# Layer matmuls of 384 instead of 288 columns in an attention, ELU and Mish kernel on one Trainium2 core

## The chip, the cores and the metric

The kernel runs on one core of a Trainium2 chip. The time is the device time of one execution in microseconds (us), lower is better. The engines are called by the names of the profile: PE is TensorE (matmuls; PEld its weight loads), DVE is VectorE, ACT is ScalarE, POOL is GpSimd, SP is SyncE, which only issues DMAs here.

## The reference

Rotary attention, then two expert layers on its output; all in float32, with weights given in float64.

```python
q, k, v: (2, 8, 576, 64)                       # batch, heads, tokens, head size
scores = rotate(q) @ rotate(k)^T / 8           # rotary table on both
attn = softmax(scores); x = attn @ v           # x: (1152, 512), tokens of both batches
h = x @ w_in                                   # (1152, 2048)
g = where(h > 0, h, exp(min(h, 0)) - 1)        # ELU
x = g @ w_out                                  # (1152, 512)
h = x @ w_in2                                  # second layer
g = h * tanh(log1p(exp(h)))                    # Mish
out = g @ w_out2
```

## The kernel before

**Numbers.** Each float32 operand of a layer matmul is split into a high and a low part (float32r), and a product is made of three passes: high x high, high x low, low x high. `XH`, `XL` hold the layer input, transposed (features on partitions). Weights come in float64 and are rebuilt on the chip: `weight_stages` takes one [128, 512] block through L95 (POOL), L99, L103, L107 (DVE), then the high part on ACT (L121) and the low part on POOL (L122). One call of `weight_part` is one of four steps of one block; `weight_job` is a whole block.

**Attention.** Eight pairs of heads (`p`), nine units each (`u = 9 p + i`): scores into PSUM (`do_S`, L407), row minima on DVE (`do_max`, L414), exponentials on ACT (`do_exp`, L427), transposes of the result on PE (`do_T`, L474, L476, L479) three units later (`LAG`), evacuated by `do_evac` and `do_evac_last`, then products with v (`do_av`, L514). The loop over `u` issues everything in a hand-written order, which every engine keeps. Row sums are inverted on DVE (`do_inverse`, into the tile `rw`), spread over partitions by transposes (`do_spread`) and copied by ACT (`do_keep`, L459); `do_x` multiplies, `do_xh` (ACT) and `do_xl` (POOL) make the parts of x. For pair 1, `second_split` makes the high parts of key and query on ACT and the low parts on POOL (L332), at units 5 and 6. The last transpose of pair 0 (L476) goes into a corner of the tile `psA`, from which `do_keep` reads; it stands at the start of unit 11.

**Layers.** G1 (`g1_mm`, L186) multiplies one block of 128 hidden features with 576 tokens of one batch, as two matmuls of 288 columns for each of 4 input blocks and 3 passes: 24 matmuls. There are 16 feature blocks x 2 batches = 32 such units a layer, in groups of four blocks. `elu` (three functions on ACT), `elu_join` (two steps on DVE, the second reads PSUM), `elu_hi` (ACT) and `elu_lo` (DVE, L238) make the two parts of g; `mish` does the same in the second layer. G2 of the first layer (`g2_first`, L779) adds a group of four feature blocks into one output block and one batch: 24 matmuls of 288 columns, 32 of them. G2 of the second layer (`g2_second`, L808) has tokens as output rows, 128 a tile, 12 matmuls of 512 columns; the tile that spans both batches needs its g parts copied together (`seam`, SP DMAs into `GX`). `step(n)` issues a unit: G1, weight steps, the functions, and one or two due G2s from `pend`. The order is by hand in the first layer; in the second only ACT's is. PSUM holds two G1 tiles and two G2 tiles of two banks; unit 4 of the first layer borrows a G2 tile. The first three G1s (`early`) are issued from the last attention units (`tail`), and `PARTS` says how many weight steps each of these units carries.

Of the kernel before, what the change touches and what calls it, by code (L numbers as in the profile page):

```python
# [14 lines left out]
ALU = mybir.AluOpType  # L15
# [11 lines left out]
def kernel(  # L27
# [31 lines left out]
    XH = main.tile([128, NB, NC, S], F32R, name="XH")  # L59
    XL = main.tile([128, NB, NC, S], F32R, name="XL")  # L60
# [24 lines left out]
    def weight_stages(key):  # L85
# [28 lines left out]
        pool, tag = wpool if even else late_pool[0], ("wi", "wo")[kind] + ("0" if even else "1")  # L114
        hi = pool.tile([128, 512], F32R, tag=tag + "h", name=tag + "h", bufs=GF)
        lo = pool.tile([128, 512], F32R, tag=tag + "l", name=tag + "l", bufs=GF)
# [58 lines left out]
    def g1_mm(m, f, b):  # L175
        c = m * NF + f
        hi, lo = WI[c]
        if (m, f, b) == (0, 0, 1):
            o = g_pool[0].tile([128, 2, 512], F32, tag="g", name="ps_g", bufs=2)
        else:  # L180
            o = ps_s()
        k = 0
        for cc in range(NC):
            for w, x in ((hi, XH), (hi, XL), (lo, XH)):
                for j in range(2):
                    nc.tensor.matmul(  # L186
                        o[:, j, :HS], lhsT=w[:, cc, :], rhs=x[:, b, cc, j * HS:j * HS + HS],
                        start=(k == 0), stop=(k == 3 * NC - 1),
                    )
                k += 1  # L190
        return o
# [7 lines left out]
    def tmp(tag):  # L199
        return late_pool[0].tile([128, S], F32, tag=tag, name=tag, bufs=5)  # L200

    def tmps():
        if tmp_pool[0] is not None:
            t = tmp_pool[0].tile([128, 2, S], F32, tag="P", name="P", bufs=PB)
            return t[:, 0, :], t[:, 1, :]
        return tmp("ta"), tmp("tb")

    def galloc(m, f, b):
# [3 lines left out]
        t = pool.tile([128, 2, S], F32R, tag=tag, name=tag, bufs=bufs)  # L212
        G[m * NF + f, b] = t
        return t[:, 0, :], t[:, 1, :]
# [4 lines left out]
    def elu(m, f, b, o):  # L219
        h = o[:, :, :HS]  # L220
# [4 lines left out]
        return m, f, b, h, t, g  # L225

    def elu_join(m, f, b, h, t, g):
        nc.vector.scalar_tensor_tensor(out=g, in0=t, scalar=1.0, in1=g, op0=ALU.add, op1=ALU.mult)  # L228
        nc.vector.tensor_tensor(out=v2(g), in0=v2(g), in1=h, op=ALU.max)  # L229
        return m, f, b, g  # L230

    def elu_hi(m, f, b, g):
        gh, gl = galloc(m, f, b)
# [7 lines left out]
    def attention(att, ps, tail):  # L241
# [3 lines left out]
        rw = att.tile([128, 4, 64], F32, name="rw")  # L245
# [82 lines left out]
        def second_split(i):  # L328
# [3 lines left out]
            nc.gpsimd.tensor_tensor(out=d[l], in0=qk_t[1][:, i, :], in1=plain(d[h]), op=ALU.subtract)  # L332
# [100 lines left out]
        def do_inverse(p, g):  # L433
# [13 lines left out]
        def do_spread(p, g):  # L447
            for t in range(2):
                nc.tensor.transpose(  # L449
                    psA[:, 128 * t:128 * t + 128], rw[:, 2 * t:2 * t + 2].rearrange("p h d -> p (h d)"), idn  # L450
# [164 lines left out]
        PARTS.update({NU: 4, NU + 1: 3, NU + 2: 2, NU + 3: 1})  # L615
# [19 lines left out]
        for u in range(max(av_at) + 1):  # L635
# [17 lines left out]
            if first_T:  # L653
# [40 lines left out]
            if u == TPP + 1:  # L694
# [4 lines left out]
                av_at[u + 1] = []  # L699
            if 0 <= u - LAG < NU:  # L700
# [20 lines left out]
            if u == 6:  # L721
# [20 lines left out]

    def moe(mp, early):
        GX = {}

        def seam(m, f, b):
            c = m * NF + f
            n = S % 128
            if b == 0:
                GX[c] = mp.tile([128, 2, 128], F32R, tag="gx", name="gx", bufs=2 * GF)  # L750
# [217 lines left out]
```

## Time and profile before

| | us |
|---|---|
| three runs | 566.83, 564.95, 564.42 |
| median | 564.95 |
| the profiled execution | 564.36 |
| its span, first to last instruction | 562.5 |
| PE busy / DVE busy / ACT busy / POOL busy | 550.6 / 369.2 / 274.6 / 237.5 |
| mean granted clock of TensorE | 0.996 |

The stages by the time of the span: the head and the two pairs that are treated apart until about 45 us, the other pairs until about 147, the first layer with ELU until about 350, the second with Mish to the end. A matmul's record is longer than its turn, as matmuls are pipelined; the turn is read from the distance between starts, or from a piece of the chain of waits that says how many matmuls it holds.

### The profile page before, as it was taken

To read this page: it belongs to the slowest core of one execution; us is meant where nothing else is said; L and a number is where in the kernel's file an instruction comes from. 1 tells how busy PE (TensorE), PEld (TensorE's weight loads), DVE (VectorE), ACT (ScalarE), POOL (GpSimd) and SP (SyncE) were. 2 spreads that over 40 slices of the span, in tenths; PEclk is the share of its full clock that TensorE was granted. 3 is DMA by queue.
4 is the path that set the end of the run, shared out by engine and by line. 5 is a ranking of instruction groups with operands and counts; after the bars stand their busy time and mean duration, and the time that the engine had idled before them with its cause. 6 is when DMAs were issued, how large, how long until landed. Compare 5 with 4: busy or idle time off the path is not lost.

```text
span 562.5 us, 10157 instructions
## 1 busy us (share of the span) xinstructions
PE 550.6 (98%) x3904; PEld 505.5 (90%) x3904; DVE 369.2 (66%) x596; ACT 274.6 (49%) x511; POOL 237.5 (42%) x231
## 2 busy tenths in 40 slices
PE   7989999999999999999999999999999999999997
PEld 6768888888899999999999999999999999999985
DVE  4758787788978866777777777679744555532231
ACT  3657676677676655455454565336443232322110
POOL 7999989843424323222332222526423322320000
PEclk9989999999999999999999999999999999999999
DMA  7378887772323232222322222425523323000012
GB/s 233 107 214 220 215 209 195 196 182 78 124 76 114 89 100 77 75 76 81 108 76 76 75 76 76 122 82 163 170 85 92 119 85 122 10 15 9 29 65 94
DMA packets 57968, 62.00 MB, mean 110 GB/s; under 512 B 29632, under 2 KB 47808, under 8 KB 57152
## 3 DMA queue, kind: packets, MB, share of 16 engines
q1 hardware_dynamic: 57376, 60.77, 37.1%
q8 instruction: 31, 0.51, 0.4%
q10 hardware_dynamic: 544, 0.59, 0.3%
q14 instruction: 17, 0.14, 0.1%
HBM read 47.51 MB, written 2.36 MB: 89 GB/s over the span
## 4 chain that ended last, share of the span: by engine, by line
PE 87%; DVE 6%; ACT 3%; issue 1%; DMA 1%; POOL 0%; SPq 0%; DVEq 0%; ACTq 0%; POOLq 0%
PE ps_s L186 32%; PE ps_h L808 18%; PE ps_g L779 17%; PE ps_s L407 8%; PE psA L514 7%; PE psT L474 5%; ACT P L427 1%; DVE wu L107 1%; DMA qk_t<-in_qk_dram 1%; DVE wu L103 1%; DVE tb L229 1%; DVE mn L414 1%; DVE tb L228 1%; PE psA L449 1%; PE psL L479 0%
## 5 line engine op out<-in xcount | busy, mean ns | idle before, releaser
L414 DVE TENSOR_REDUCE mn<-ps_s 128x1 f32<-128x576 f32 x72 | 53.6, 754 | 23.1 <-PE ps_s L407 22.8
L758 ACT ACTIVATE ta<-ps_s 128x576 f32<-128x576 f32 x32 | 20.8, 649 | 94.2 <-PE ps_s L186 94.1
L427 ACT ACTIVATE P<-ps_s,mn 128x576 f32<-128x576 f32 x72 | 53.1, 740 | 10.9 <-DVE mn L414 10.6
L186 PE MATMUL ps_s<-XL,wi1h 128*128 128x288 f32 x256 | 54.9, 296 | 0.0
L186 PE MATMUL ps_s<-XH,wi1h 128*128 128x288 f32 x256 | 54.7, 295 | 0.0
L186 PE MATMUL ps_s<-XH,wi1l 128*128 128x288 f32 x256 | 54.6, 295 | 0.0
L186 PE MATMUL ps_s<-XH,wi0h 128*128 128x288 f32 x248 | 53.6, 298 | 0.6 <-DVE tb L229 0.5
L186 PE MATMUL ps_s<-XL,wi0h 128*128 128x288 f32 x248 | 53.2, 296 | 0.0
L186 PE MATMUL ps_s<-XH,wi0l 128*128 128x288 f32 x248 | 53.0, 295 | 0.0
L122 POOL TENSOR_TENSOR wo0l<-wu,wo0h 128x512 fp32r<-128x512 f32 x16 | 21.8, 1364 | 68.7 <-ACT wo0h L121 58.1
L99 DVE TENSOR_SCALAR wu<-wu 128x512 int32<-128x512 int32 x64 | 29.4, 460 | 31.8 <-POOL wu L95 31.8
L107 DVE SCALAR_TENSOR_TENSOR wu<-raw,wu 128x512 int32<-128x512 int32 x64 | 47.3, 740 | 1.8
L103 DVE SCALAR_TENSOR_TENSOR wu<-raw,wu 128x512 int32<-128x512 int32 x64 | 47.1, 736 | 2.0
L122 POOL TENSOR_TENSOR wi0l<-wu,wi0h 128x512 fp32r<-128x512 f32 x16 | 21.4, 1340 | 63.7 <-ACT wi0h L121 63.7
L95 POOL TENSOR_SCALAR wu<-raw 128x512 f32<-128x512 f32 x64 | 44.8, 702 | 4.8
L122 POOL TENSOR_TENSOR wo1l<-wu,wo1h 128x512 fp32r<-128x512 f32 x16 | 22.0, 1375 | 58.3 <-ACT wo1h L121 58.3
L760 DVE TENSOR_TENSOR g<-ta,g 128x576 fp32r<-128x576 f32 x25 | 20.4, 817 | 36.4 <-ACT g L759 36.4
L122 POOL TENSOR_TENSOR wi1l<-wu,wi1h 128x512 fp32r<-128x512 f32 x16 | 21.4, 1334 | 53.3 <-ACT wi1h L121 53.3
L474 PE MATMUL psT<-idn,P 128*128 128x128 f32 x288 | 43.5, 276 | 0.0
L186 PEld LDWEIGHTS ps_s<-XH,wi1h 128*128 128x128 f32 x256 | 42.0, 188 | 1.2
L186 PEld LDWEIGHTS ps_s<-XH,wi0h 128*128 128x128 f32 x248 | 40.3, 188 | 2.8 <-DVE tb L229 1.0
L228 DVE SCALAR_TENSOR_TENSOR tb<-ta,tb 128x576 f32<-128x576 f32 x30 | 22.7, 757 | 29.6 <-ACT tb L224 29.3
(176 smaller groups left out, 1454.9 us busy)
## 6 DMA issues: line engine op xcount, KB each, us to landing
raw<-in_w_in_dram SPq DMA_DIRECT2D x32, 512.0 KB, 3.8
raw<-in_w_out_dram SPq DMA_DIRECT2D x32, 512.0 KB, 3.3
qk_t<-in_qk_dram SPq DMA_DIRECT2D x6, 1152.0 KB, 5.3
qa<-qh SPq DMA_DIRECT2D x24, 144.0 KB, 3.7
out_dram<-Y SPq DMA_DIRECT2D x9, 256.0 KB, 2.0
ka<-kh SPq DMA_DIRECT2D x12, 144.0 KB, 3.2
ka<-kl SPq DMA_DIRECT2D x12, 144.0 KB, 2.6
qb<-ql SPq DMA_DIRECT2D x12, 144.0 KB, 3.1
```

Of the source, the lines that this page charges most:

```text
L95: nc.gpsimd.tensor_scalar(out=u, in0=high.bitcast(F32), scalar1=REBASE, scalar2=0.0, op0=ALU.mult, op1=ALU.add)
L103: nc.vector.scalar_tensor_tensor(out=ui, in0=high, scalar=-0x80000000, in1=ui, op0=ALU.bitwise_and, op1=ALU.bitwise_or)
L107: nc.vector.scalar_tensor_tensor(out=ui, in0=low, scalar=29, in1=ui, op0=ALU.logical_shift_right, op1=ALU.bitwise_or)
L122: nc.gpsimd.tensor_tensor(out=lo, in0=u, in1=plain(hi), op=ALU.subtract)
L186: nc.tensor.matmul(o[:, j, :HS], lhsT=w[:, cc, :], rhs=x[:, b, cc, j * HS:j * HS + HS], start=(k == 0), stop=(k == 3 * NC - 1),)
L407: nc.tensor.matmul(psS[w][:, j, :HS], lhsT=l, rhs=r(slice(j * HS, j * HS + HS)), start=(a == 0), stop=(a == len(passes) - 1),)
L414: nc.vector.tensor_reduce(out=m, in_=psS[u][:, :, :HS], axis=AX.XY, op=ALU.min)
L427: nc.scalar.activation(out=P.rearrange("p (j n) -> p j n", j=2), in_=psS.pop(u)[:, :, :HS], func=AF.Exp, scale=-1.0, bias=mn_t.pop(u), acc ...
L474: nc.tensor.transpose(tv[:, c, :], P[:, k:k + 128], idn)
L514: nc.tensor.matmul(o[64 * h:64 * h + 64, cols], lhsT=v, rhs=rhs, start=(c == 0 and first), stop=(c == 4), skip_group_check=True,)
L779: nc.tensor.matmul(o[:, j, :HS], lhsT=w[:, e * 128:e * 128 + 128], rhs=gt[:, i, j * HS:j * HS + HS], start=(k == 0), stop=(k == 3 * GF - 1),)
L808: nc.tensor.matmul(o, lhsT=l, rhs=w, start=(k == 0), stop=(k == 3 * GF - 1))
```

## The change

The layers are cut in three chunks of 384 tokens instead of two batches of 576. A G1 unit is a pair of feature blocks with one chunk: the two PSUM banks of a tile hold the two blocks, and each matmul has 384 columns. That makes 8 pairs x 3 chunks = 24 units of 24 matmuls a layer. `g2_first` has a chunk and a pair of output blocks, 24 times. The chunks are multiples of 128, so `seam` and `GX` go. `XH`, `XL` become [128, 4, 1152]; the g tiles and the temporaries are 768 wide, and half of the even W_out blocks' tiles move to the later pool. `count(n)` and `due(n)` say how many weight blocks a step carries: 0, 0, 2, 1, 2, 2, then one and two in turn. The third early unit reads tokens of the second batch.

In the attention, pair 1's low parts go to DVE (`second_lo`, at units 5 and 7, with `stack_q(1)` at 7), pair 0's last transpose is issued at the end of unit 10, `rw` becomes a part of the tile `R_t`, and the low part of x for pair 0 goes to DVE.

```diff
-    XH = main.tile([128, NB, NC, S], F32R, name="XH")
+    XH = main.tile([128, NC, NT], F32R, name="XH")
...
-    def g1_mm(m, f, b):
-        c = m * NF + f
-        hi, lo = WI[c]
-        if (m, f, b) == (0, 0, 1):
-            o = g_pool[0].tile([128, 2, 512], F32, tag="g", name="ps_g", bufs=2)
-        else:
-            o = ps_s()
+    def g1_mm(m, fp, t):
+        o = ps_s()
+        ws = [WI[m * NF + 2 * fp + j] for j in range(2)]
         k = 0
         for cc in range(NC):
-            for w, x in ((hi, XH), (hi, XL), (lo, XH)):
+            for i, x in ((0, XH), (0, XL), (1, XH)):
                 for j in range(2):
                     nc.tensor.matmul(
-                        o[:, j, :HS], lhsT=w[:, cc, :], rhs=x[:, b, cc, j * HS:j * HS + HS],
+                        o[:, j, :CH], lhsT=ws[j][i][:, cc, :], rhs=x[:, cc, t * CH:t * CH + CH],
                         start=(k == 0), stop=(k == 3 * NC - 1),
                     )
...
             nc.scalar.activation(out=d[h], in_=qk_t[1][:, i, :], func=AF.Copy)
-            nc.gpsimd.tensor_tensor(out=d[l], in0=qk_t[1][:, i, :], in1=plain(d[h]), op=ALU.subtract)
+
+        def second_lo(i):
+            d = sp_t[1]
+            h, l = ("kh", "kl") if i else ("qh", "ql")
+            nc.vector.tensor_tensor(out=d[l], in0=qk_t[1][:, i, :], in1=plain(d[h]), op=ALU.subtract)
...
-        PARTS.update({NU: 4, NU + 1: 3, NU + 2: 2, NU + 3: 1})
+        PARTS.update({NU: 4, NU + 1: 2, NU + 2: 1, NU + 3: 1})
...
-            if first_T:
+            if first_T and u != TPP + 2:
                 do_T(u - LAG)
...
                 av_at[u + 1] = []
+                do_T(u + 1 - LAG)
...
-            if u == 6:
+            if u in (5, 7):
+                second_lo(2 if u == 5 else 0)
+            if u == 7:
                 stack_q(1)
...
-                    do_xl(pp, g, nc.gpsimd if pp < NP - 1 else nc.vector)
+                    do_xl(pp, g, nc.gpsimd if 0 < pp < NP - 1 else nc.vector)
...
+    units = [(m, g * GF // 2 + k, t) for m in range(2) for g in range(NG) for t in range(NT // CH) for k in range(GF // 2)]
...
-        def g2_first(g, b, e):
+        def g2_first(g, t, ep):
...
-                for w, i in ((hi, 0), (hi, 1), (lo, 0)):
+            for f in range(g * GF, g * GF + GF):
+                for w, i in ((0, 0), (0, 1), (1, 0)):
                     for j in range(2):
+                        e = 2 * ep + j
                         nc.tensor.matmul(
-                            o[:, j, :HS], lhsT=w[:, e * 128:e * 128 + 128], rhs=gt[:, i, j * HS:j * HS + HS],
+                            o[:, j, :CH], lhsT=WO[f][w][:, e * 128:e * 128 + 128], rhs=g_part(f, t, i),
...
+        def due(n):
+            return 2 * GF + (n + 1) * 2 * GF // (UB * NT // CH)
+
+        def count(n):
+            if n < half - 1:
+                return (0, 0, 2, 1, 2, 2)[n] if n < 6 else 1 + n % 2
+            return max(0, min(len(jobs), due(n)) - njob[0])
...
             if m == 0:
-                for _ in range(3 if GF <= n < half - 1 else 0):
-                    weight_part()
+                if n >= GF - 1:
+                    some(3)
                 if o is not None:
-                    o = elu(m, f, b, o)
-                    for _ in range(3 if n < GF else 0):
-                        weight_part()
+                    o = elu(units[n], o)
+                    some(8 if n == 2 else 0)
                     o = elu_join(*o)
-                if GF <= n < half - 1:
-                    weight_part()
+                some(1)
                 if o is not None:
                     o = elu_hi(*o)
+                some(3)
             else:
-                mish(m, f, b, o)
-            if f % GF == GF - 1:
-                g = f // GF
+                mish(units[n], o)
+            if fp % UB == UB - 1:
+                g = fp // UB
                 if m == 0:
-                    pend.extend((n + (2 if n < GF else D1 if n < half - 1 else LATE[e]), (0, (g, b, e))) for e in range(NC))
+                    pend.extend((n + 2, 0, g, t, ep) for ep in range(NC // 2))
                 else:
-                    pend.extend((n + D2, (1, (g, t))) for t in TB[b])
-            cnt = 2 if n in (2 * GF, half - 2, half + 1, half + 2) or n > half and n % 8 == 4 else 1
+                    pend.extend((n + 2, 1, g, t * CH // 128 + i) for i in range(CH // 128))
+            cnt = 2 if n > half + 2 and n % 2 else 1
```

## Rows read from the trace of the kernel before

**Rows 1.** The page, engine shares: busy us, share of the span, instructions.
```profile
PE 550.6 (98%) x3904; PEld 505.5 (90%) x3904; DVE 369.2 (66%) x596; ACT 274.6 (49%) x511; POOL 237.5 (42%) x231
```
**Rows 2.** Windows: from:to us, busy PE, PEld, DVE, ACT, POOL, clock, DMA, GB/s.
```profile
20.00:40.00 20.00, 17.89 (x148) 13.16 (x149) 12.38 (x25) 11.65 (x28) 19.32 (x17) 0.91 0.56 155
...
184.60:345.00 160.40, 160.40 (x1205) 160.40 (x1204) 119.48 (x175) 85.93 (x134) 50.07 (x50) 1.00 0.27 86
377.30:539.60 162.30, 162.30 (x974) 148.12 (x973) 82.13 (x116) 53.27 (x87) 47.40 (x44) 1.00 0.27 80
539.60:562.50 22.90, 19.02 (x84) 15.40 (x82) 5.57 (x8) 1.33 (x2) 0.00 (x0) 0.97 0.23 84
```
**Rows 3.** Waits of PE: who waited for whom, us in total, times, longest.
```profile
PE psA L476 <- ACT R L459: 2.1, 1, 2.1
...
PE ps_s L186 <- DVE tb L229: 0.5, 1, 0.5
```
**Rows 4.** The chain of waits in the layers: start, us, what.
```profile
197.37 3.20 PE ps_s L186 x24
200.57 3.20 PE ps_g L779 x24
...
430.18 3.18 PE ps_s L186 x24
433.36 2.74 PE ps_h L808 x12
```
**Rows 5.** Groups of DVE by form: busy us, mean ns, idle before and releaser.
```profile
L107 DVE SCALAR_TENSOR_TENSOR wu<-raw,wu 128x512 int32<-128x512 int32 x64 | 47.3, 740 | 1.8
...
L99 DVE TENSOR_SCALAR wu<-wu 128x512 int32<-128x512 int32 x64 | 29.4, 460 | 31.8 <-POOL wu L95 31.8
L228 DVE SCALAR_TENSOR_TENSOR tb<-ta,tb 128x576 f32<-128x576 f32 x30 | 22.7, 757 | 29.6 <-ACT tb L224 29.3
L238 DVE TENSOR_TENSOR g<-tb,g 128x576 fp32r<-128x576 f32 x24 | 22.5, 939 | 8.1 <-ACT g L234 6.9
```
**Rows 6.** Timeline where the first layer begins, PE and POOL: start, us, what.
```profile
158.01 0.53 PE L186 MATMUL ps_s<-XH,wi0h 128*128 128x288 f32 x2
...
169.91 1.29 POOL L122 TENSOR_TENSOR wo0l<-wu,wo0h 128x512 fp32r<-128x512 f32 x1 [2.69 <-ACT wo0h L121]
...
170.90 0.69 PE L779 MATMUL ps_g<-ge,wo0h 128*128 128x288 f32 x4
```
**Rows 7.** Timeline of PE in the head, in brackets idle time before and releaser.
```profile
28.34 0.61 PE L474 MATMUL psT<-idn,P 128*128 128x128 f32 x4
31.02 0.30 PE L476 MATMUL psA<-idn,P 128*64 128x128 f32 x1 [2.07 <-ACT R L459]
...
36.33 0.53 PE L407 MATMUL ps_s<-kh,qa 64*128 64x288 f32 x4
```
**Rows 8.** Windows, 32 to 36 us, with the granted clock behind the five engines.
```profile
32.00:36.00 4.00, 4.00 (x25) 2.47 (x22) 2.26 (x4) 1.55 (x4) 3.84 (x4) 0.57 0.62 220
```
**Rows 9.** Timeline of DVE and ACT in the head.
```profile
20.94 1.42 DVE L414 TENSOR_REDUCE mn<-ps_s 128x1 f32<-128x576 f32 x2 [0.68 <-PE ps_s L407]
...
30.05 0.59 ACT L494 ACTIVATE pt<-psT 128x512 f32<-128x512 f32 x1
...
30.84 0.43 ACT L541 ACTIVATE XH<-R 128x256 fp32r<-128x256 f32 x1
...
32.35 1.42 DVE L414 TENSOR_REDUCE mn<-ps_s 128x1 f32<-128x576 f32 x2
```
**Rows 10.** Timeline of DVE at the end of the attention: steps with two SBUF inputs.
```profile
148.66 1.02 DVE L103 SCALAR_TENSOR_TENSOR wu<-raw,wu 128x512 int32<-128x512 int32 x1
...
151.90 0.84 DVE L545 TENSOR_TENSOR XL<-R,XH 128x256 fp32r<-128x256 f32 x1 [0.62 <-ACT XH L541]
...
161.65 0.52 DVE L545 TENSOR_TENSOR XL<-R,XH 128x320 fp32r<-128x320 f32 x1 [0.54 <-ACT XH L541]
```

More of the change, by code (lines that the diff above doesn't have):

```diff
@@ L113, in weight_stages @@
         even = c // GF % 2 == 0
-        pool, tag = wpool if even else late_pool[0], ("wi", "wo")[kind] + ("0" if even else "1")
-        hi = pool.tile([128, 512], F32R, tag=tag + "h", name=tag + "h", bufs=GF)
-        lo = pool.tile([128, 512], F32R, tag=tag + "l", name=tag + "l", bufs=GF)
+        tag, bufs = ("wi", "wo")[kind] + ("0" if even else "1"), GF
+        if kind and even:
+            bufs = GF // 2
+            tag += "b" * (c % GF >= bufs)
+        pool = wpool if even and tag[-1] != "b" else late_pool[0]
+        hi = pool.tile([128, 512], F32R, tag=tag + "h", name=tag + "h", bufs=bufs)
+        lo = pool.tile([128, 512], F32R, tag=tag + "l", name=tag + "l", bufs=bufs)
         if kind == 0:
@@ L211, in galloc, with g_part, elu @@
         pool, tag, bufs = (main, "ge", GE) if i < GE else (late_pool[0], "g", GB - GE)
-        t = pool.tile([128, 2, S], F32R, tag=tag, name=tag, bufs=bufs)
-        G[m * NF + f, b] = t
-        return t[:, 0, :], t[:, 1, :]
+        g = pool.tile([128, 2, 2 * CH], F32R, tag=tag, name=tag, bufs=bufs)
+        G[m, fp, t] = g
+        return g[:, 0, :], g[:, 1, :]
+    def g_part(f, t, i):
+        m, f = divmod(f, NF)
+        return G[m, f // 2, t][:, i, f % 2 * CH:f % 2 * CH + CH]
     def v2(t):
         return t.rearrange("p (j n) -> p j n", j=2)
-    def elu(m, f, b, o):
-        h = o[:, :, :HS]
+    def elu(unit, o):
+        h = o[:, :, :CH]
         t, g = tmps()
@@ L449, in do_spread @@
                 nc.tensor.transpose(
[L450 removed]
+                    psA[:, 128 * t:128 * t + 128], R_t[p, g][:, 128 * t:128 * t + 128], idn
                 )
@@ L816, in g2_second @@
                     nc.sync.dma_start(out=out[t * 128:t * 128 + 128, :], in_=y)
-        blocks = [(m, g, b) for m in range(2) for g in range(NG) for b in range(NB)]
-        g1_seq = [(m, g * GF + fi, b) for m, g, b in blocks for fi in range(GF)]
-        half = len(g1_seq) // 2
-        D1, D2, LATE = 1, 2, (2, 2, 3, 3)
+        half = len(units) // 2
+        UB = GF // 2
         pend = []
+        late_pool[0] = mp
         def run_g2(it):
-            if it[0] == 0:
-                g2_first(*it[1])
-            else:
-                g2_second(*it[1])
@@ L836, in step, with some @@
+        def step(n):
+            m, fp, t = units[n]
+            o = early.pop(n) if n in early else g1_mm(m, fp, t)
+            todo = 4 * count(n) if n < half - 1 else 0
+            def some(k):
+                nonlocal todo
+                for _ in range(min(k, todo)):
+                    weight_part()
+                    todo -= 1
             if m == 0:
-                for _ in range(3 if GF <= n < half - 1 else 0):
-                    weight_part()
+                if n >= GF - 1:
+                    some(3)
@@ L857, in step @@
+            cnt = 2 if n > half + 2 and n % 2 else 1
             while pend and cnt and pend[0][0] <= n:
-                run_g2(pend.pop(0)[1])
+                run_g2(pend.pop(0)[1:])
                 cnt -= 1
-            if m == 0:
-                if o is not None:
-                    elu_lo(*o)
-            for _ in range(0 if n < half - 1 else 1 + (n in (half + 1, half + 2))):
-                weight_job()
+            if m == 0 and o is not None:
+                elu_lo(*o)
+            some(4)
@@ L866, in moe @@
+            if n >= half - 1:
+                for _ in range(count(n)):
+                    weight_job()
         pools = ExitStack()
@@ L880, in moe @@
             for n in range(half, 2 * half):
-                if n == half + 4:
+                if n == half + 3:
                     psum("ps_h")
```

95 lines of the change are left out of this document (36 added, 59 removed).

## The prediction

> **What bounds the kernel now.** I read the engine shares first: TensorE is busy 98% of the span, VectorE 66% [rows 1]. An average says little, so next came the stages. In 184.6 to 345 us (first layer) and in 377.3 to 539.6 us (second layer) TensorE is busy for the whole stretch at the full granted clock; VectorE has 119.5 of 160.4 us there, and 82.1 of 162.3. Only the head (20 to 40 us: 17.9 of 20, clock 0.91) and the last stretch leave gaps [rows 2]. The waits of TensorE agree: two matter here, 2.1 us once in the head, and 0.5 us once where the first layer begins [rows 3]. So outside the head the kernel lasts as long as its matmuls take from start to start. That pitch is read from the chain of waits, since the duration of one record contains pipeline time: 24 matmuls of 288 columns take 3.20 us in the first layer, 3.18 us in the second, and 12 of 512 columns take 2.74 us [rows 4]. Per matmul: 133.3, 132.5 and 228.3 ns.
>
> **The matmuls.** At 2.4 GHz, where these stretches run, 288 columns last 120.0 ns and 512 last 213.3 ns, so 13.3 and 15.0 ns come on top of the columns. A line through the two measured pitches has a slope of 0.424 ns per column and 11 ns at zero columns; 384 columns then cost 133.3 + 96 x 0.424 = 174.0 ns in the first layer and 173.3 in the second. No row has 384 columns: the bounds are 160 + 13.3 and 160 + 15.0. I take the line, as it lies between two rows of the same kind of matmul.
> The change keeps the columns and cuts the matmuls by a quarter. G1 (L186) has 64 units of 24 before and 48 of 24 after, half of them in each layer; the first layer's G2 (L779) has 32 x 24 = 768 before and 24 x 24 = 576 after; the second layer's G2 (L808) stays at 432.
> First layer G1: 768 x 133.3 = 102.4 us becomes 576 x 174.0 = 100.2. Its G2: the same, 102.4 to 100.2. Second layer G1: 768 x 132.5 = 101.8 becomes 576 x 173.3 = 99.8. Sum: 306.6 to 300.2, or 6.4 us less. With the bounds: 1728 matmuls at 173.3 to 175.0 ns give 299.5 to 302.4, a gain of 7.1 to 4.2 us. All of it lies on the path, since TensorE has no gap there.
> The Trainium skill speaks against a gain of this size: its page "TensorE: Matmul & The Clock Gate", section "Back-to-back issue gap", gives N / 2.4 GHz + 2.5 ns for a warm matmul. By that, dropping 576 matmuls is worth 1.4 us, not 6.4. The rows show 13.3 and 15.0 ns above the columns where the page has 2.5, each of these matmuls with a weight load of its own; the trace disagrees with the page here.
>
> **VectorE and ScalarE in the layers.** A unit is now 768 wide instead of 576, and there are three for four. I scale the rows by 4/3, which is an upper bound because the fixed part of an instruction doesn't grow: 757 to 1009 ns for the join (two of them), 939 to 1252 for the low part [rows 5], and 1000 for adding a G2 result. One unit of the first layer: 2 x 1.01 + 1.25 + 1.00 = 4.3 us. The weights come faster: between units 6 and 22 the new count gives 25 weights to 17 units, 1.47 each, at 460 ns and twice 740 ns (L103 has the form of L107) = 1.94 us [rows 5], or 2.85 us. Together 7.1 us of a unit's TensorE time of 48 x 174 ns = 8.35 us: 85%. The waits for ScalarE between max and low part fall mostly under the weight steps placed there. A unit's PSUM tile is wanted again two units later, 12.5 us after its G1 ended, and G2 wants the unit two units on, so VectorE may lag by several us before TensorE notices: no cost. The seam copies (one SP DMA per second-layer unit) go; nothing on the path waited for them: no gain.
>
> **Where the layers begin.** Units 0 and 1 last 24 x 174 ns = 4.18 us each after and 3.20 before, so the attention's last products slip by 1.95 us; unit 2, at 158.0 before [rows 6], starts near 159.9, unit 3 ends two units later near 168.3, and the first G2 follows at once; before, it started at 170.9 [rows 6]. So the fourth W_out weight is due earlier than before, when its low part began at 169.9 on GpSimd [rows 6]. I followed the queues, with the durations of the trace scaled to 768 (an estimate): ScalarE starts unit 1 near 158.0, after unit 0's high part, and is through its three functions at 160.5; two joins on VectorE, to 162.4; the last x product, its copy and unit 1's high part, to 164.2; its low part, to 165.2; then the last two weights at 1.94 us each, to 169.0. ScalarE's high part of the last one ends near 169.6, and GpSimd's low part takes 1.29 us from there [rows 6], behind the opening of the next weight: near 171.4. G2 takes the weights in order and reaches this low part after 22 of its 24 matmuls, at 168.3 + 22 x 0.174 = 172.1. It fits, by 0.7 us; a late weight costs its lateness, up to 2 us. The PSUM tile of unit 2 is free near 170.9 (two joins behind the weights) and wanted by unit 4 at 172.5. The third PSUM pool, which unit 4 borrowed, isn't needed: before, the 0.5 us wait was for such a tile [rows 3]; I let it go, 0.45 us. Between the layers, unit 24 needs the first chunk's sum, high and low part: about 3.1 us of VectorE and ScalarE after the chunk's last G2, while one G1 and one G2 (8.3 us) lie between: hidden. The end stays: last product, one add, one DMA [rows 2].
>
> **The head.** Before, pair 0's last transpose goes to psA, behind ScalarE's copy from psA, and TensorE stands from 28.95 to 31.02 us [rows 7]; the clock then is 0.57 between 32 and 36 us [rows 8]. The change issues this transpose one step earlier, ahead of that copy, so the 2.07 us go. What is late next? The scores of the next two tiles need the PSUM tiles that the exponentials free, and these end at 29.96 us (ScalarE's evacuation starts at 30.05 [rows 9]); so at best 1.2 us.
> Against that stand new waits on VectorE. The key's low part enters its queue ahead of the row minima that start at 20.94 us [rows 9], and the query's ahead of the next ones. No row shows this instruction on VectorE. The 576-wide low part of the layers takes 939 ns [rows 5], and a 256-wide one took 0.84 us while GpSimd worked, a 320-wide one 0.52 us while it didn't [rows 10]: between 0.76 and 1.5 us; I take 1.2, nearer the contended row, as GpSimd is busy 19.3 of these 20 us [rows 2]. Two of them, half of it in idle time, delay the following pair's minima by some 1.2 us. Then pair 0's low part of x (L545) moves to VectorE too: it waits for ScalarE's copy of 30.84 us (now near 32.0), and behind it stand the evacuation of the last transpose and the minima that began at 32.35. They begin near 34.3; products, exponentials and the scores of 36.33 us [rows 7] follow at 36.6. Net +0.3 us, if the clock holds; if it falls again the half-rate products add about 1.5 us, and if VectorE isn't slowed the head gains up to 2 us. I take +0.3, with -2 to +2. GpSimd is relieved, but in the list from which [rows 3] are taken no line of TensorE names it.
> The Trainium skill names the reason for the contended row: "GPSIMD Engine Reference" (introduction, table of the engine) says that GpSimd shares its SBUF interfaces with VectorE and contends with VectorE instructions that have two SBUF inputs, as both low parts have. With the uncontended price the sum would be about 1 us lower.
>
> **The sum.** The profiled execution took 564.36 us (span 562.5 and 1.9 around it), 0.6 below the median of 564.95. 564.36 - 6.4 - 0.45 + 0.3 = 557.8; I say 558.0.
>
> **The rivals.**
> (a) The change doesn't do what it says: what comes on top of the columns grows with them (13.3 x 384 / 288 = 17.8 ns, pitch 177.8, sum 307.2 and thus no gain), 564.2 with the other terms. Against it: 15.0 and not 23.7 ns at 512 columns. Chance 0.08. The page on TensorE named above would have it in a milder form, 562.8.
> (b) The head loses the clock again, and the layers' start waits up to 2 us for its weights: 558 + 1.5 + 2 = 561.5, and past 562.1 if the matmuls give only their lower bound as well. The margin of 0.7 us speaks for it, and the clock that fell in the head before [rows 8]. Chance 0.12.
> (c) Slower: VectorE becomes the bound of the first layer, because its weights come in 17 units instead of being spread. Place: units 6 to 22; it decides when a unit costs VectorE more than 8.35 us. All of its two-input steps at the contended rate (1.02 us for a weight step, as the one at 148.66 us [rows 10]) make 1.47 x 2.5 + 4.7 = 8.4 us, and 0.5 to 0.9 us of waits for ScalarE that nothing fills make about 9.2: 17 x 0.85 = 14 us, or 572. Against it: the means of [rows 5], which already hold this mix. Chance 0.06.
> The forecast has 0.74, with its own range from 564.36 - 7.1 - 0.45 - 2 = 554.8 to 564.36 - 4.2 - 0.45 + 2 = 561.7.
>
> **How the numbers follow.** The range takes in the forecast and three quarters of (b), about 0.83: 554.8 to 562.0. A measurement of this kernel tells about 0.5% (2.8 us) from no change, so faster means below 562.1: the forecast and three quarters of (b), 0.83; the same: (a) and the rest of (b), 0.11; slower: (c), 0.06.
>
> **What would show it.** Right: 3328 matmuls; in the chain 24 matmuls of 384 columns take 4.17 to 4.18 us in both layers; no wait of TensorE between 145 and 540 us above 0.5 us; the transpose to psA ahead of the copy, with the scores of 36.33 us within 2 us of that place. Wrong: 24 matmuls at 4.27 us (a), TensorE waiting for a wo0 weight near 172 us or at a clock below 1 after 32 us (b), or TensorE waiting for VectorE's max in every unit of the first layer (c).

## The result, and the profile after

| | before, us | after, us |
|---|---|---|
| median of the runs beside each other | 564.95 | 560.17 |
| lowest and highest | 564.42 to 566.83 | 558.71 to 561.32 |
| profiled execution, and its span | 564.36, 562.5 | 561.02, 559.2 |

The ratio is 0.9904, with a 95% interval from 0.9874 to 0.9934: faster by 1%, 2.2 us above the 558.0 of the prediction and inside its range. Executions of one kernel lie some 2 us apart, in part because TensorE's granted clock falls in the head of some of them; the profiled execution of the changed kernel is one of those.

The page of the changed kernel, engine shares (busy us, share of the span, instructions), for [rows 1]:

```profile
PE 546.1 (98%) x3328; PEld 500.5 (90%) x3328; DVE 375.8 (67%) x560; ACT 267.4 (48%) x459; POOL 244.4 (44%) x227
```

Its windows (from:to us, busy PE, PEld, DVE, ACT, POOL, clock, DMA share, GB/s), for [rows 2] and [rows 8]:

```profile
20.00:40.00 20.00, 16.61 (x124) 12.31 (x125) 13.32 (x22) 10.43 (x26) 15.38 (x13) 0.84 0.57 156
184.60:345.00 160.40, 160.40 (x928) 160.40 (x927) 136.65 (x162) 87.44 (x115) 65.39 (x58) 1.00 0.30 96
377.30:539.60 162.30, 162.30 (x825) 148.12 (x824) 72.67 (x101) 47.56 (x67) 43.56 (x40) 1.00 0.19 61
...
32.00:36.00 4.00, 2.19 (x17) 1.66 (x16) 3.78 (x6) 1.00 (x4) 3.57 (x3) 0.70 0.93 335
36.00:40.00 4.00, 4.00 (x24) 2.63 (x21) 0.36 (x1) 1.34 (x4) 0.52 (x1) 0.50 0.83 179
```

The layers are still solid TensorE. VectorE is busy for 136.7 of 160.4 us of the first layer, 85%, which is what the prediction said. The head lost: 16.6 us of TensorE work in 20 to 40 us where there were 17.9, at a mean clock of 0.84. From 36 to 40 us the clock is 0.50, the lower of its two levels, and TensorE, busy all that time, starts 24 matmuls.

The waits of TensorE (who waited for whom, us in total, times, longest), for [rows 3]:

```profile
PE ps_s L415 <- ACT P L435: 3.2, 7, 0.9
PE psA L521 <- DVE pt L499: 1.8, 1, 1.8
...
PE ps_g L777 <- POOL wo0bl L127: 0.8, 1, 0.8
PE ps_g L777 <- ACT wo0bh L126: 0.3, 1, 0.3
```

The 2.1 us for ScalarE's copy and the 0.5 us for a PSUM tile are gone. In their place stand 1.8 us for `pt` in the head and 0.8 + 0.3 = 1.1 us for weights where G2 begins. The waits for the exponentials (`P`) have grown as well, from 1.8 us in 4 waits to 3.2 in 7: 0.90 us at 24.11 us, 0.17 and 0.33 near 31 us.

The chain of waits in the layers (start, us, what), for [rows 4]:

```profile
181.50 4.16 PE ps_g L777 x24
185.66 4.16 PE ps_s L187 x24
...
494.63 4.18 PE ps_s L187 x24
498.82 2.76 PE ps_h L801 x12
```

A matmul of 384 columns takes 4.16 / 24 = 173.3 ns in the first layer and 4.18 / 24 = 174.2 ns in the second. The 1536 matmuls of the first layer at 133.3 ns [rows 4] were 204.8 us and are 1152 at 173.3, 199.7; those of the second layer's G1 go from 101.8 to 576 x 174.2 = 100.3. Together 6.6 us less.

From the first G1 (146.82 us before, 149.73 after) to the end of the span the kernel takes 562.5 - 146.82 = 415.7 us before and 559.2 - 149.73 = 409.5 after: 6.2 us gained. The head gives 149.73 - 146.82 = 2.9 us back. That is the whole difference, 564.36 - 6.2 + 2.9 = 561.1. Some tenths in such places belong to the execution and not to an edit: the first scores start at 9.30 us before and at 9.50 after, and with one and the same head at 9.19 (e4_TL, below) and 9.39 (e7_TLparts).

### The profile page after: what moved, and what is told of

It reads as the page before. It is cut to its first block, busy times and chain, and to the rows that moved or that the text cites. A ratio compares the mean times of both kernels' runs of the same rounds, so it can differ in the third digit from the quotient of the medians.

```text
span 559.2 us, 8818 instructions
## 1 busy us (share of the span) xinstructions
PE 546.1 (98%) x3328; PEld 500.5 (90%) x3328; DVE 375.8 (67%) x560; ACT 267.4 (48%) x459; POOL 244.4 (44%) x227
## 4 chain that ended last, share of the span: by engine, by line
PE 87%; DVE 3%; POOL 3%; issue 3%; DMA 2%; ACT 1%; SPq 0%; POOLq 0%; ACTq 0%
PE ps_s L187 33%; PE ps_h L801 18%; PE ps_g L777 17%; PE ps_s L415 7%; PE psA L521 7%; PE psT L481 4%; DMA qk_t<-in_qk_dram 1%; DVE mn L422 1%; DMA bh<-qa 1%; ACT P L435 1%; POOL wu L96 1%; POOL wo0bl L127 1%; POOL wo0l L127 1%; PE psL L486 0%; DVE wu L108 0%
## 5 line engine op out<-in xcount | busy, mean ns | idle before, releaser
L100 DVE TENSOR_SCALAR wu<-wu 128x512 int32<-128x512 int32 x64 | 39.7, 620 | 43.1 <-POOL wu L96 43.1
L759 ACT ACTIVATE ta<-ps_s 128x768 f32<-128x768 f32 x24 | 19.5, 812 | 100.8 <-PE ps_s L187 100.8
L104 DVE SCALAR_TENSOR_TENSOR wu<-raw,wu 128x512 int32<-128x512 int32 x64 | 50.6, 791 | 2.0
L187 PE MATMUL ps_s<-XH,wi0h 128*128 128x384 f32 x192 | 49.1, 336 | 0.0
L108 DVE SCALAR_TENSOR_TENSOR wu<-raw,wu 128x512 int32<-128x512 int32 x64 | 47.8, 747 | 1.8
L187 PE MATMUL ps_s<-XL,wi1h 128*128 128x384 f32 x192 | 48.9, 335 | 0.0
L187 PE MATMUL ps_s<-XL,wi0h 128*128 128x384 f32 x192 | 48.8, 335 | 0.0
L187 PE MATMUL ps_s<-XH,wi1l 128*128 128x384 f32 x192 | 48.8, 335 | 0.0
L187 PE MATMUL ps_s<-XH,wi0l 128*128 128x384 f32 x192 | 48.8, 335 | 0.0
L187 PE MATMUL ps_s<-XH,wi1h 128*128 128x384 f32 x192 | 48.7, 334 | 0.0
L761 DVE TENSOR_TENSOR g<-ta,g 128x768 fp32r<-128x768 f32 x16 | 17.5, 1093 | 37.0 <-ACT g L760 37.0
L501 ACT ACTIVATE pt<-psT 128x512 f32<-128x512 f32 x44 | 26.2, 597 | 28.9 <-PE psT L481 28.9
L521 PE MATMUL psA<-pt,v_t 128*64 128x256 f32 (+1 forms) x240 | 37.1, 410 | 2.3 <-DVE pt L499 1.8
L481 PEld LDWEIGHTS psT<-idn,P 128*128 128x128 f32 x288 | 35.2, 143 | 2.0 <-issue 1.4
```

The costliest lines, as they stand in the source:

```text
L100: nc.vector.tensor_scalar(out=ui, in0=ui, scalar1=3, scalar2=0x7FFFFFF8, op0=ALU.logical_shift_left, op1=ALU.bitwise_and)
L104: nc.vector.scalar_tensor_tensor(out=ui, in0=high, scalar=-0x80000000, in1=ui, op0=ALU.bitwise_and, op1=ALU.bitwise_or)
L108: nc.vector.scalar_tensor_tensor(out=ui, in0=low, scalar=29, in1=ui, op0=ALU.logical_shift_right, op1=ALU.bitwise_or)
L187: nc.tensor.matmul(o[:, j, :CH], lhsT=ws[j][i][:, cc, :], rhs=x[:, cc, t * CH:t * CH + CH], start=(k == 0), stop=(k == 3 * NC - 1),)
L481: nc.tensor.transpose(tv[:, c, :], P[:, k:k + 128], idn)
L521: nc.tensor.matmul(o[64 * h:64 * h + 64, cols], lhsT=v, rhs=rhs, start=(c == 0 and first), stop=(c == 4), skip_group_check=True,)
```

## The experiments

The edits of the head are called L (pair 1's low parts on VectorE, `stack_q(1)` at unit 7), T (pair 0's last transpose at the end of unit 10; with it `rw` inside `R_t`) and X (pair 0's low part of x on VectorE). The kernels ran in three groups (e1 to e4; e5 and e7 to e9; e11 to e13), each on one chip beside the kernel before (medians there 564.25, 564.39 and 564.57 us).

| kernel | head | weight shares | median, us | range | ratio to before, 95% |
|---|---|---|---|---|---|
| e1_layers | as before | 4, 2, 1, 1 | 560.21 | 558.13 to 560.44 | 0.989 to 0.995 |
| e2_T | T | 4, 2, 1, 1 | 558.34 | 558.05 to 558.53 | 0.987 to 0.993 |
| e3_TX | T, X | 4, 2, 1, 1 | 558.62 | 558.34 to 560.78 | 0.988 to 0.994 |
| e4_TL | T, L | 4, 2, 1, 1 | 557.01 | 556.53 to 557.22 | 0.985 to 0.991 |
| e8_L | L | 4, 2, 1, 1 | 558.88 | 557.34 to 559.33 | 0.987 to 0.991 |
| e13_after | L, T, X | 4, 2, 1, 1 | 559.22 | 558.85 to 560.27 | 0.988 to 0.993 |
| e11_Xlate | L, T, X later | 4, 2, 1, 1 | 557.38 | 556.93 to 557.58 | 0.984 to 0.990 |
| e12_Xlate_parts | L, T, X later | 4, 3, 1 | 556.32 | 556.14 to 556.84 | 0.982 to 0.988 |
| e7_TLparts | T, L | 4, 3, 1 | 555.95 | 555.78 to 557.06 | 0.983 to 0.987 |
| e9_head | L, T, X, layers as before | 4, 3, 2, 1 | 566.19 | 564.43 to 568.49 | 1.002 to 1.005 |
| e5_192 | L, T, X, G1 in 192 columns | 4, 2, 1, 1 | 614.99 | one run | |

**Layers alone, and the head edits one by one.** The changed kernel with L, T and X undone (e1_layers), then T (e2_T), T and X (e3_TX), T and L (e4_TL) put in again. The lines of L and X, undone:

```diff
-            nc.vector.tensor_tensor(out=d[l], in0=qk_t[1][:, i, :], in1=plain(d[h]), op=ALU.subtract)
+            nc.gpsimd.tensor_tensor(out=d[l], in0=qk_t[1][:, i, :], in1=plain(d[h]), op=ALU.subtract)
...
-                    do_xl(pp, g, nc.gpsimd if 0 < pp < NP - 1 else nc.vector)
+                    do_xl(pp, g, nc.gpsimd if pp < NP - 1 else nc.vector)
```

> The layers of the changed kernel with the attention of the kernel before (low parts of pair 1 and of pair 0's x on GpSimd, last transpose of pair 0 after the copy from psA, the tile rw). Theory: the layers alone gain 6.9 us and lose 0.7 to late weights, and the new head is a loss of 1 to 3 us by the execution: 558.0 to 558.8, so 1.5 to 2.5 us under the changed kernel (560.2). Rival: the head is neutral and the layers gave less than drawn: the same as the changed kernel, 560 to 561.

> The changed kernel with only one of its edits of the head left, the earlier transpose; both kinds of low parts are back on GpSimd. Theory: without the new VectorE steps the wait of 2.07 us goes and the scores of the next two tiles start when the exponentials allow it, 1 us earlier than before, and the clock holds: 555.5 to 557.5. Rival: the transpose is worth nothing, since the exponentials come next: as the layers alone, 558 to 559.

> The changed kernel with pair 1's low parts back on GpSimd; the earlier transpose and pair 0's low part of x on VectorE stay. Theory: the low part of x waits on VectorE for ScalarE's copy near 31.3 us and the products with v behind it start near 33, 1.5 us earlier than in the changed kernel; TensorE still stands for about 1 us there, so the clock may fall: 556.5 to 559.5. If the low parts of pair 1 alone are the loss, this is as fast as the transpose alone.

> The changed kernel with pair 0's low part of x back on GpSimd; pair 1's low parts stay on VectorE. Theory: both new steps share the loss; the low parts delay the row minima by 0.9 us, but the queue then isn't held by ScalarE's copy, the products start near 32.5 instead of 34.6 and the clock holds: 556.5 to 558.5. If the low parts of pair 1 are the whole loss: 560, as the changed kernel.

Measured: 560.21, 558.34, 558.62 and 557.01 us. T and L without X (e4_TL) beat the changed kernel by 2.2 us (e13_after, on another chip) to 3.2 us (560.17), inside its expectation. The expectations of e1_layers and e2_T missed at the median, and their rivals had it. Of e1_layers only the three executions at mean clocks of 0.997 to 1.000 took the expected time, 558.1 to 558.2 us. e3_TX is as fast as e2_T within 0.3 us: without L, X shows no clear cost. What T alone does is seen where pair 1's last transposes begin. In e1_layers TensorE still stands for 2.06 us near 29 us, in e2_T it doesn't, and yet the layers start at 146.85 us in the one and at 147.24 in the other (0.33 of these 0.39 us stand already at the first scores). A later wait takes the time, 1.37 us in e1_layers and 1.60 in e2_T. The timeline of e1_layers, and the last line for e2_T (start, us, engine, line, what, in brackets idle before and releaser), show it:

```profile
46.61 0.88 POOL L550 TENSOR_TENSOR XL<-R,XH 128x320 fp32r<-128x320 f32 x1
47.53 0.65 DVE L448 TENSOR_SCALAR R<-twice,rc 128x64 f32<-128x64 f32 x1 [1.86 <-POOL XL L550]
49.09 0.41 DVE L509 COPY pl<-psL 128x256 f32<-128x256 f32 x1
49.56 0.30 PE L481 MATMUL psL<-idn,P 128*64 128x128 f32 x1 [1.37 <-DVE pl L509]
...
49.94 0.30 PE L479 MATMUL psL<-idn,P 128*64 128x128 f32 x1 [1.60 <-DVE pl L507]
```

VectorE writes `R` again, so it waits for GpSimd's low part of x to have read it; behind it stands `pl`, and TensorE waits for that. GpSimd is hardly idle there (7.84 of the 8 us from 40 to 48 us busy), so its queue sets the time. The kernel before has the same end of GpSimd's step, 47.45 against 47.49 us, though its clock fell at 32 us [rows 8] and that of e1_layers didn't:

```profile
46.58 0.87 POOL L545 TENSOR_TENSOR XL<-R,XH 128x320 fp32r<-128x320 f32 x1
47.48 0.66 DVE L443 TENSOR_SCALAR R<-twice,rc 128x64 f32<-128x64 f32 x1 [0.30 <-POOL XL L545]
...
49.54 0.27 PE L476 MATMUL psL<-idn,P 128*64 128x128 f32 x1
```

Here TensorE comes to these transposes at 49.54 us without a wait, in e1_layers at 49.56 us after a wait of 1.37. So in the kernel before two paths end level at this place. One is TensorE's own, with the 2.07 us of [rows 7] and the products at the fallen clock; the chain that ended last runs through them (start, us, what):

```profile
33.35 2.33 PE psA L514 x10
```

The other is GpSimd's. Time taken off TensorE's path alone gains nothing there, as e2_T shows, and the fallen clock cost nothing beyond GpSimd's end. L takes two steps off GpSimd. In e4_TL its low part of x starts at 45.52 us, TensorE's wait shrinks to 0.27, and the layers start at 145.76:

```profile
45.52 0.87 POOL L552 TENSOR_TENSOR XL<-R,XH 128x320 fp32r<-128x320 f32 x1
46.43 0.42 DVE L448 TENSOR_REDUCE R<-rc 128x256 f32<-128x256 f32 x1 [1.21 <-POOL XL L552]
...
48.46 0.30 PE L483 MATMUL psL<-idn,P 128*64 128x128 f32 x1 [0.27 <-DVE pl L511]
```

L has a price of its own. In the changed kernel the key's low part takes 1.75 us on VectorE, the minima behind it begin at 22.39 instead of 20.94 us, and TensorE waits 0.90 us for their exponentials (0.88 in e4_TL, none in e1_layers):

```profile
20.71 1.75 DVE L340 TENSOR_TENSOR kl<-qk_t,kh 128x576 fp32r<-128x576 f32 x1 [0.26 <-ACT kh L335]
...
24.11 0.54 PE L415 MATMUL ps_s<-kh,bh 128*128 128x288 f32 x2 [0.90 <-ACT P L435]
```

What L gains is net of this.

**L without T.** e4_TL with the transpose put back.

```diff
-            if first_T and u != TPP + 2:
+            if first_T:
...
-                do_T(u + 1 - LAG)
```

> Layers as changed, and of the edits of the head only pair 1's low parts on VectorE; the transpose of pair 0 stays where it was, so TensorE's wait of 2.07 us for ScalarE's copy stays too. Theory, GpSimd's queue sets the end of the head: in e1_layers and e2_T the unit 0 of the layers starts at 146.85 and 147.24 us, with and without that wait, since VectorE then waits for GpSimd's low part of x at 46.6 to 47.0 us; with the low parts off GpSimd it is 145.76 in e4_TL. Then the low parts alone bring it: unit 0 at 145.8 to 146.0, time 557.0 to 557.3, as e4_TL. Rival, the wait of TensorE is worth its length once GpSimd is relieved: unit 0 at 147 or later, 558.2 to 559, and e4_TL owes its gain to both.

Measured: 558.88 us, nearer to the rival. One of its five executions took 557.34, at a mean clock of 1.000: there L alone is within 0.4 us of e4_TL. The other four took 558.7 to 559.3 at 0.995 to 0.997. The profiled one is of these. TensorE stands for 1.84 us, then the windows from 28 to 40 us are:

```profile
28.00:32.00 4.00, 2.16 (x22) 1.64 (x20) 2.14 (x6) 2.67 (x7) 3.84 (x5) 1.00 0.60 127
32.00:36.00 4.00, 4.00 (x28) 2.65 (x28) 2.88 (x5) 1.55 (x4) 3.80 (x4) 0.62 1.01 340
36.00:40.00 4.00, 4.00 (x40) 3.12 (x39) 1.90 (x5) 1.71 (x4) 3.46 (x3) 0.95 0.99 234
```

and the layers start at 147.41 us, 1.65 later than in e4_TL. So L moves the bound, and T then removes the wait behind which the clock fell here. That the clock makes the difference between the fast execution and the others rests on their mean clocks and this one trace; e4_TL ran on another chip.

**X: its place in the queue.** In the changed kernel X's first step stands in VectorE's queue ahead of `pl`, `pt` and the minima. The timeline of the changed kernel:

```profile
31.95 1.40 POOL L324 TENSOR_TENSOR kl<-qk_t,kh 128x576 fp32r<-128x576 f32 x1
32.22 1.41 DVE L552 TENSOR_TENSOR XL<-R,XH 128x256 fp32r<-128x256 f32 x1 [1.81 <-ACT XH L548]
33.56 0.27 DVE L511 COPY pl<-psA 64x128 f32<-64x128 f32 x1
33.76 0.67 DVE L499 COPY pt<-psT 128x512 f32<-128x512 f32 x1
34.35 1.40 DVE L422 TENSOR_REDUCE mn<-ps_s 128x1 f32<-128x576 f32 x2
34.58 0.77 PE L521 MATMUL psA<-pt,v_t 128*64 128x320 f32 x1 [1.80 <-DVE pt L499]
38.16 0.85 PE L415 MATMUL ps_s<-kh,qa 64*128 64x288 f32 x4
```

It waits for ScalarE's `XH`, then takes 1.41 us for 256 columns beside GpSimd, and TensorE stands 1.80 us for `pt`. The next run moves this one instruction behind the minima and leaves it on VectorE; the changed kernel ran beside it.

```diff
-                    do_xl(pp, g, nc.gpsimd if 0 < pp < NP - 1 else nc.vector)
+                    if (pp, g) != (0, 0):
+                        do_xl(pp, g, nc.gpsimd if 0 < pp < NP - 1 else nc.vector)
+            if u == TPP + 2:
+                do_xl(0, 0, nc.vector)
```

> The changed kernel with one instruction moved in VectorE's queue: the low part of x of pair 0's first group, which stood ahead of the copies pl and pt and the maximum, now stands behind them. Theory, place in the queue: in the changed kernel this step waited for ScalarE's XH and then for GpSimd (1.41 us for 256 columns), pl and pt stood behind it and TensorE waited 1.80 us for pt. Behind them it delays nobody before its slack of 2 us is used: no wait for pt above 0.3 us, unit 0 of the layers at 145.8 us, 557.0 +- 0.5 us. Rival, the step costs wherever it stands, since it holds up GpSimd or the next copy of pt on VectorE: a wait of TensorE near 36 us or unit 0 past 147, 558.5 to 560.

> The changed kernel itself, unchanged, beside e11_Xlate and e12_Xlate_parts on one chip: 558.7 to 561.3 us as before, TensorE waiting 1.80 us for pt at 34.6 us. In an execution in which the granted clock stays at its upper level behind that wait I expect unit 0 at about 147.5 instead of 149.73 us and some 558.7 us.

Measured: 557.38 against 559.22 us. The place is what X cost, 1.8 us by these medians. At the later place the step also takes 0.41 us instead of 1.41 (the last section says why). In e11_Xlate TensorE waits 0.17 us for `pt`, and the layers start at 145.63 us:

```profile
32.70 0.45 PE L521 MATMUL psA<-pt,v_t 128*64 128x320 f32 x1 [0.17 <-DVE pt L499]
...
33.81 0.41 DVE L552 TENSOR_TENSOR XL<-R,XH 128x256 fp32r<-128x256 f32 x1
33.82 1.68 POOL L324 TENSOR_TENSOR ql<-qk_t,qh 128x576 fp32r<-128x576 f32 x1
```

The profiled execution of e13_after has the same 1.80 us of waiting at a clock that held. The scores that start at 38.16 us above start at 36.51 here, and the layers at 147.81 instead of 149.73:

```profile
34.57 0.45 PE L521 MATMUL psA<-pt,v_t 128*64 128x320 f32 x1 [1.80 <-DVE pt L499]
...
36.51 0.80 PE L415 MATMUL ps_s<-kh,qa 64*128 64x288 f32 x4
```

and in its windows the clock is

```profile
32.00:36.00 4.00, 2.20 (x21) 1.46 (x19) 3.78 (x6) 1.01 (x4) 3.57 (x3) 1.00 0.93 325
```

So X in its place costs 147.81 - 145.63 = 2.2 us, of which 0.3 stand already at the first scores (9.51 and 9.23 us), and the fallen clock 1.9 more.

**The late weights.** T and L, with one weight step moved from unit NU + 3 to unit NU + 1 of those that end the attention (e7_TLparts), and the same with X later (e12_Xlate_parts).

```diff
-        PARTS.update({NU: 4, NU + 1: 2, NU + 2: 1, NU + 3: 1})
+        PARTS.update({NU: 4, NU + 1: 3, NU + 2: 1})
```

> The change without its step on x in pair 0 (as in e4_TL, 557.01 us), and with one weight step moved from the seventh of the units that end the attention to the second: shares 4, 3, 1 instead of 4, 2, 1, 1. Late weights: the wait of TensorE at the first G2s (0.27 for wo0bh and 0.81 for wo0bl in the changed kernel, 1.1 us together) goes or falls below 0.4 us, and the time is 556.0 +- 0.4. Rival, VectorE and PSUM: unit 2's max ended at 176.5 us there and unit 4 wanted its tile at 175.5, so taking the weight wait away only uncovers 0.5 to 1 us of waiting for the tile, and the time stays at 556.7 to 557.2. A second rival: the step moved forward delays the joins of units 0 and 1 by its 2.5 us on VectorE; 557.5.

> As e11_Xlate, with the weight steps shared 4, 3, 1 as in e7_TLparts (555.95 us). If both effects add up: 557.0 - 1.0 = 556.0. If the low parts of x on VectorE also free GpSimd for the wait that is left in the head (0.27 us for pl in e4_TL): 555.6. Rival as in e11_Xlate: 557.5 to 559.

Measured: 555.95 and 556.32 us, against 557.01 (another chip) and 557.38 (the same). Both waits for `wo0b` weights are gone, and no other came in their place. e7_TLparts has the lowest median, 0.9847 of the kernel before (0.9827 to 0.9867), 3.3 us below e13_after and 4.2 below the first runs of the changed kernel, on other chips. (The expectation says the seventh unit and means NU + 3.) In the changed kernel the rows of ScalarE, VectorE and GpSimd show why the weights were late:

```profile
167.58 0.83 ACT L239 ACTIVATE ge<-qk_t 128x768 fp32r<-128x768 f32 x1
168.31 0.62 ACT L126 ACTIVATE wo0h<-wu 128x512 fp32r<-128x512 f32 x1
...
172.52 1.67 DVE L108 SCALAR_TENSOR_TENSOR wu<-raw,wu 128x512 int32<-128x512 int32 x1
...
174.22 0.63 ACT L126 ACTIVATE wo0bh<-wu 128x512 fp32r<-128x512 f32 x1 [2.31 <-DVE wu L108]
174.93 1.71 POOL L127 TENSOR_TENSOR wo0bl<-wu,wo0bh 128x512 fp32r<-128x512 f32 x1 [0.23 <-ACT wo0bh L126]
...
176.69 0.62 PE L777 MATMUL ps_g<-ge,wo0bl 128*128 128x384 f32 x2 [0.81 <-POOL wo0bl L127]
```

The high part of an earlier W_out weight stands behind unit 1's high part of g on ScalarE. In e7_TLparts it stands ahead of it, at 161.29 us, 2.3 us after unit 2's G1 began (159.00); in the changed kernel that distance is 168.31 - 162.91 = 5.4 us. The chain of the last two weights then hangs on it. Steps of VectorE and GpSimd that hold each other up lengthen this chain further: L108 at 172.52 us takes 1.67 us, 0.69 elsewhere in the same stretch (163.24 us), and the last low part 1.71.

**The head edits alone.** L, T and X on the layers of before.

> The layers of the kernel before (288 columns), with all edits of the head as in the changed kernel. If the parts add up and the step on x in pair 0 is what the head lost: unit 0 at about 149.7 us where TensorE's clock falls after the wait of 1.8 us for pt, and near 148 where it doesn't, so 564.4 + 2.9 = 567.3 or some 565.5 us; a ratio of 1.002 to 1.006 to the kernel before. As my prediction had it (+0.3 us): 564.7. If the layers' new units are what loses time at their start and the head gains: below 563.

Measured: 566.19 us, 1.003 of the kernel before (1.0015 to 1.0046). The head as changed loses. In the profiled execution, 564.43 us, the clock held and the layers start at 146.98 us, 0.16 after the kernel before, with the same 1.78 us for `pt`; those at mean clocks of 0.988 to 0.997 took 565.9 to 568.5. At the median the loss is 1.8 us, between the 0.2 of this execution and the 2.9 of the changed kernel's profiled one; the expected place of 148 us at a held clock was 1 us too late.

**The turn of a matmul.** Each G1 matmul of the changed kernel split into two of 192 columns.

```diff
-                    nc.tensor.matmul(
-                        o[:, j, :CH], lhsT=ws[j][i][:, cc, :], rhs=x[:, cc, t * CH:t * CH + CH],
+                    for q in range(0, CH, 192):
+                        nc.tensor.matmul(
+                            o[:, j, q:q + 192], lhsT=ws[j][i][:, cc, :], rhs=x[:, cc, t * CH + q:t * CH + q + 192],
```

> The changed kernel with each G1 matmul of 384 columns of both layers split into two of 192, each with its own weight load: 2304 instead of 1152, the same columns. Line through the measured turns (133.3 ns at 288, 173.3 at 384 columns, so 13.3 ns + 0.4167 ns a column): 93.3 ns a matmul, 48 in 4.48 us instead of 24 in 4.16, so 48 x 0.32 = +15 us, 575 us. Turns proportional to the columns: no change, 560. A floor by the weight load, the transposes of 128 columns standing 110 ns apart: 48 in 5.28 us, +54 us, 614 us.

Measured: 614.99 us, the floor. The chain of waits holds 48 of them in 5.34 us (first fence), and each of these matmuls has its own weight load (second fence, one group of the weight loads: busy us, mean ns; a record overlaps the next):

```profile
179.30 5.34 PE ps_s L188 x48
```

```profile
L188 PEld LDWEIGHTS ps_s<-XL,wi0h 128*128 128x128 f32 x384 | 50.6, 192 | 0.0
```

That is 111.3 ns a turn, where the line gives 93.3. The added cost is 1152 x (2 x 111.3 - 173.3) = 56.8 us, and 55 were measured. So the turn isn't proportional to the columns, and the line doesn't reach down to 192: below some length a floor sets the turn. The load of the next weights is the likely floor; no run here separates it from another fixed cost of a matmul. The Trainium skill, "TensorE: Matmul & The Clock Gate", section "LDWEIGHTS (loading the stationary operand)", gives a weight load of P columns P / 1.2 ns, 107 ns at 128; the turn measured here agrees within 5 ns.

## Why the prediction came out as it did

**The whole.** The sum of 558.0 us was 2.2 us too low, and the time lies inside the range because three quarters of rival (b) had been let into it. By the prediction's own signs (b) is what came in the profiled execution: a wait of 0.81 us for a wo0 weight, and a clock of 0.50 after 36 us. Its 561.5 us lies 0.5 from the 561.02 of that execution. In e13_after, where the clock held, half of (b) came.

**The matmuls: right.** 6.6 us measured, 6.4 predicted; the turn of 173.3 to 174.2 ns lies within 1 ns of the line through 288 and 512 columns. The Trainium skill, "TensorE: Matmul & The Clock Gate", section "Back-to-back issue gap", would have given 1.4 us with its N / 2.4 GHz + 2.5 ns, a rate that the section states for an isolated matmul; the runs don't bear it out for these streams. Rival (a) is out by these turns; its own was 177.8 ns.

**VectorE in the layers: right that it doesn't bind, and the 85% in part by luck.** 136.7 of 160.4 us, and after unit 4 TensorE waits for nothing. The scaled durations were upper bounds, as said: the two joins took 975 and 954 ns (1009), the low part 1093 (1252). But the weight steps were priced too low. From 184.6 to 345 us L100 took 784 ns on average, L104 901 and L108 692, together 2.4 us a weight where the prediction had 1.94; in the same stretch of the kernel before they took 414, 693 and 693. The two errors largely cancel. Rival (c) did not come.

**Where the layers begin: wrong by 1.1 us.** The step that failed is "it fits, by 0.7 us". The 0.45 us for the PSUM tile went, as said. But I placed the weight steps by VectorE's work alone and let ScalarE's high parts follow at once; one stands behind a high part of g that waits for a join. GpSimd's low part was priced at 1.29 us from an undisturbed row and took 1.54 to 1.71, and a step of VectorE took 1.67 us instead of 0.69. Rival (b) named this wait.

**The head: wrong by 0.7 to 2.6 us.** The parts of it:
- The order of the last transpose: right as a step. It ran at 29.96 us without a wait, and the next scores waited for the exponentials (0.17 and 0.33 us), as predicted.
- The low parts of L: the price of 1.2 us each was too low for the key's (1.75 us, beyond the bound of 1.5) and near for the query's (1.06). The forecast delay of some 1.2 us came: the minima begin at 22.39 instead of 20.94 us, with 0.2 of it from the first scores.
- X: its mechanism was in the text, the evacuation and the minima behind it, to start near 34.3 us (measured 34.35) and the next scores at 36.6 (36.51 where the clock held). The place they were compared with was wrong. The 36.33 us of [rows 7] belongs to an execution whose clock had fallen; with the clock held the same program has them at 34.78 us (e1_layers). So the way to these scores became 36.51 - 34.78 = 1.7 us longer, where I had read 0.3. With GpSimd relieved, 147.81 - 146.85 = 1.0 of it is left where the layers start.
- "GpSimd is relieved, but in the list no line of TensorE names it" is the step that failed. That list has one link only, and only the path that ends last. One link back VectorE waits for GpSimd's XL until 47.48 us; that path ended level with TensorE's own, and it set the end of the head as soon as TensorE's was shorter (e1_layers, e2_T). L on top of T was worth 1.3 us (e4_TL against e2_T, 557.0 against 558.3), which X spent again.

The fall of the clock, priced at 1.5 us in rival (b), cost 1.9 us in the changed kernel (149.73 against 147.81); in the kernel before it cost nothing, since GpSimd's path ended level. With the measured terms the sum is 564.36 - 6.6 - 0.45 + 1.1 + 2.9 = 561.3 for the profiled execution (561.02 measured), and 1.9 less, 559.4, where the clock holds (559.09 in e13_after). Each of the two misses went the same way, and the larger gain of the matmuls didn't cover them.

What stays open: why the clock falls in one execution and not in another. Seven profiled executions have a wait of TensorE of 1.78 us or more near 30 us. In four (before, after, e8_L, e5_192) the clock fell in the windows behind it, in three (e1_layers, e9_head, e13_after) it held. In the six without such a wait (e2_T, e3_TX, e4_TL, e7_TLparts, e11_Xlate, e12_Xlate_parts) it was 1.00 from 20 to 48 us. Nor is it shown why four of twelve executions of the kernel before took 560.3 to 562.5 us beside e1_layers, or where four of the seven of e1_layers, at mean clocks of 0.990 to 0.993, spent 2 us more than the profiled one: no trace is of such an execution.

## What to carry to other kernels

Fewer, longer matmuls with a weight load each saved some 11 ns for each that went (6.6 us for 576); read the turn from the chain of waits and don't extend the line to short matmuls, where a floor took over here (111 ns). A wait of TensorE that is removed is worth its length only if no other path ends level with it: follow every engine one link further back than the list of TensorE's waits, and compare only places of executions with the same clock. A share that comes out as forecast doesn't prove its terms; compare them one by one. An instruction that nobody needs soon belongs behind those that feed TensorE; moving one such instruction, and one weight step, made 1.8 and 1.1 us.

## What the runs showed of the hardware

In the places looked at here, a two-input step of VectorE and an instruction of GpSimd don't run side by side at a lower rate: the later one is held up by the other, and a step of VectorE that began second ends 0.28 us (256 columns) or 0.60 us (576) after GpSimd's. X's first step took 1.41 us in the changed kernel, 0.67 in e3_TX and 0.41 in e11_Xlate, with the same 256 columns. It ended at 32.22 + 1.41 = 33.63 us, 0.28 behind GpSimd's step (31.95 + 1.40). In e3_TX it ended at 31.36 + 0.67 = 32.03, 0.28 behind again:

```profile
30.32 1.43 POOL L300 TENSOR_TENSOR qk_t<-qk_t,tab 128x576 f32<-128x576 f32 x1
31.36 0.67 DVE L548 TENSOR_TENSOR XL<-R,XH 128x256 fp32r<-128x256 f32 x1 [1.81 <-ACT XH L544]
```

The key's low part, with 576 columns, ends 0.60 us behind GpSimd's step in the changed kernel (20.71 + 1.75 against 20.44 + 1.42), the query's 0.61. In e11_Xlate X's step began 0.01 us ahead of GpSimd's, kept its 0.41, and GpSimd's took 1.68 instead of 1.41. So the price of such a step isn't a factor on its duration, as I had taken it between 0.76 and 1.5 us: it is up to the rest of the other engine's instruction. The Trainium skill, "GPSIMD Engine Reference", section "1. Specifications", has the shared interface with VectorE instructions of two SBUF inputs; the trace agrees, by the 1.41 and 0.41 us of X's step.
